# Another order of the first block's steps, with 39 unread products of the identity between TensorE's first steps

## The chip, the cores and the metric

The kernel runs on one core of a Trainium2 chip. The metric is the device time of one execution, in microseconds (us). The engines are TensorE (PE in the profile, PEld its weight loads), VectorE (DVE), ScalarE (ACT), GpSimd (POOL) and SyncE (SP), which issues most DMA transfers.

## The reference

q, k and v have the shape [8, 8, 576, 64] (batch, heads, tokens, width). Attention stays within chunks of 64 tokens; its result, as x of 4608 tokens by 512, goes through a feed-forward layer with 2048 inner columns, mish and no bias.

```python
scores = scale * np.matmul(q_c, k_c.transpose(0, 1, 2, 4, 3))
scores = scores - np.max(scores, axis=-1, keepdims=True)
attn = np.exp(scores)
attn = attn / (np.sum(attn, axis=-1, keepdims=True) + 1e-09)
out = np.matmul(attn, v_c)
...
h = x @ w_in
sp = np.where(h > 20.0, h, np.log1p(np.exp(np.minimum(h, 20.0))))
g = h * np.tanh(sp)
return (g @ w_out).astype(np.float32)
```

All of it is fp32. The kernel keeps nearly that precision in the feed-forward layer by splitting each operand in an upper part, rounded to a shorter type that TensorE multiplies in one pass (fp32r), and a lower part, the difference. A product is then three products of parts.

## The kernel before, in words

The tokens are taken in pairs of 64-token chunks of two batches; two pairs make a block of 512 tokens by 512. The first block is special: the weights have to be loaded, split and kept while it runs, and the attention of the first two pairs has to be done before anything can be multiplied by `w_in`. Later blocks run as a steady stream of products, in which sums of operands save some of the products.

A pair `j` passes through these steps. `load_qk` (L278) and `load_v` (L286) load it. `a_scores` is a run of small products (`small_mm`, L295, 64x64, `s<-k,q`). `a_max` (L321), `a_sub` (L333), `a_inverse` (L388 to L390) and `a_norm` (L395) are softmax on VectorE; `a_exp` (L342) is on ScalarE. `a_transpose` (L406, `pt<-ident,p`) turns p over with the identity `ident` on TensorE, `a_copy` (L416, `ps<-pt`) brings it to SBUF on ScalarE, `a_values` (L295, `av<-ps`) multiplies by v. `a_hi` (L446) and `a_lo` (L449) split the result into the parts of `x_first`. For the first two pairs each step is done for one half at a time: `a_scores 0 1` is pair 0, second half.

A weight `n` passes through `load` (L107), `scale` (L120 and L125, ACT), `bits` (L139, DVE; L143 stores a copy), `hi` (L164, ACT) and `lo` (L167, DVE); `keep` (L176, L177) writes the split weight to memory for the later blocks.

The feed-forward layer of the first block: `up i` (L524, `h<-x_first,wi`) makes 128 of the 2048 inner columns for 512 tokens with 12 products; the first of them is done in two halves of 256 tokens, `up0A` (pair 0) and `up0B` (pair 1). `mish i` (L537) follows on ACT, `gh` and `gl` (L546, L548, L552) split the result, and `fill i` issues the down products (`down_mm`, L562, `o<-wo,gl` and `o<-wo,gh`) into the accumulators of `w_out`, which `open` makes room for. The steps `x`, `s_load`, `s_adds`, `s_hi` and `s_lo` prepare the next block's operands.

What sets the order is a string written out by hand, `ORDER`. `first_block` takes its steps one by one and calls `atom`, which emits each step's instructions. An engine executes its own instructions in the order of emission; between engines, only data and buffers order them. The steps after `at n` don't run there, but beside products of the next block.

Of the kernel before, what the change touches and what calls it, by code (L numbers as in the profile page):

```python
# [9 lines left out]
F32 = mybir.dt.float32  # L10
# [7 lines left out]
P = 128  # L18
CHUNK = 64
# [4 lines left out]
def kernel(  # L24
# [34 lines left out]
    at = ctx.enter_context(tc.tile_pool(name="at", bufs=3))  # L59
# [204 lines left out]
    st = {}  # L264
# [248 lines left out]
    it = {}  # L513
# [41 lines left out]
    fill = []  # L555
# [108 lines left out]
    }  # L664

    ORDER = """
        qk0, a_scores 0 0, a_max 0 0, rooms, v0, a_sub 0 0, a_exp 0 0, a_scores 0 1, a_max 0
        1, load 0, load 1, qk1, load 3, scale 0, a_inverse 0 0, a_sub 0 1, a_norm 0 0, a_exp
        0 1, a_T 0 0, bits 0, load 4, hi 0, a_scores 1 0, a_inverse 0 1, a_copy 0 0, lo 0,
        a_norm 0 1, v1, a_max 1 0, scale 1, a_sub 1 0, a_V 0 0, a_hi 0 0, bits 1, a_exp 1 0,  # L670
        load 2, a_T 0 1, a_copy 0 1, a_lo 0 0, scale 3, a_inverse 1 0, a_scores 1 1, a_max 1
        1, a_sub 1 1, a_V 0 1, a_hi 0 1, hi 1, a_norm 1 0, a_lo 0 1, up0A, a_T 1 0, a_exp 1
        1, a_inverse 1 1, scale 4, a_norm 1 1, scale 2, a_copy 1 0, a_T 1 1, bits 3, load_qk
        0, a_copy 1 1, load 5, hi 3, lo 1, keep 0, bits 2, a_V 1 0, a_hi 1 0, a_lo 1 0, a_V
        1 1, load 6, a_hi 1 1, a_lo 1 1, open, scale 5, scores 0, bits 5, up0B, mish 0, hi
        2, hi 5, bits 4, up1, lo 2, load 7, hi 4, gh 0, gl 0, lo 3, load_v 0, mish 1, max 0,
        lo 5, scale 6, fill 0, gh 1, up 2, lo 4, mish 2, scale 7, fill 1, gh 2, bits 6, gl
        1, sub 0, hi 6, bits 7, gl 2, load 8, lo 6, hi 7, lo 7, up 3, load 9, keep 1, exp 0,
        fill 2, up 4, scale 8, inverse 0, fill 3, mish 3, up 5, bits 8, gh 3, norm 0, T 0,
        load 10, gl 3, scale 9, bits 9, load 11, load_qk 1, hi 8, fill 4, mish 4, gh 4, copy  # L680
        0, lo 8, V 0, gl 4, hi 9, lo 9, fill 5, scale 10, mish 5, scale 11, up 6, up 7, bits
        10, gh 5, raw 0, bits 11, mish 6, gl 5, scores 1, hi 10, gh 6, load 12, hi 11, lo
        10, mish 7, lo 11, load_v 1, load 13, scale 12, up 8, keep 2, max 1, sub 1, gl 6,
        mish 8, exp 1, fill 6, bits 12, gh 7, scale 13, up 9, hi 12, inverse 1, fill 7, load
        14, gl 7, norm 1, bits 13, lo 12, gh 8, load_qk 2, gl 8, T 1, fill 8, copy 1, V 1,
        hi 13, scale 14, lo 13, raw 1, load 15, bits 14, load 16, up 10, mish 9, gh 9,
        scores 2, max 2, mish 10, load_v 2, sub 2, fill 9, gl 9, scale 15, hi 14, bits 15,
        lo 14, exp 2, up 11, hi 15, inverse 2, gh 10, load 17, keep 3, fill 10, norm 2, up
        12, gl 10, scale 16, T 2, load_qk 3, lo 15, x 0 0, x 0 3, x 0 4, mish 11, bits 16,
        scale 17, fill 11, copy 2, mish 12, hi 16, gh 12, bits 17, gh 11, load 18, V 2, up  # L690
        13, lo 16, x 0 2, x 0 5, gl 11, gl 12, hi 17, raw 2, scores 3, fill 12, keep 4, lo
        17, max 3, sub 3, up 14, mish 13, scale 18, bits 18, x 0 1, x 1 1, hi 18, exp 3, lo
        18, load_v 3, keep 5, s_load 1, inverse 3, fill 13, up 15, s_load 0, x 0 8, gh 13,
        mish 14, gh 14, gl 13, norm 3, mish 15, s_adds 0, keep 6, s_hi 0, x 0 6, s_load 2,
        gl 14, T 3, fill 14, ops 2, copy 3, s_lo 0, gh 15, x 1 0, gl 15, x 0 7, s_adds 1, V
        3, raw 3, x 1 2, fl 0, x 1 3, x 1 4, x 1 5, x 0 9, keep 7, ops 3, fl 1, x 1 8, at 0,
        fill 15, x 1 9, x 1 7, at 1, fl 2, fl 3, fl 4, s_hi 1, at 2, fl 5, load_qk 4, fl 6,
        x 1 6, at 3, s_lo 1, x 0 10, at 4, s_load 3, x 1 10, at 5, fl 7, st 0, at 6, at 7,
        st 1, at 8, at 9, s_adds 2, s_adds 3, at 10, s_hi 3, s_hi 2, s_lo 2, at 11, at 12,
        at 13, s_lo 3, at 14, at 15, at 16, at 17, at 18, at 19, at 20, at 21, at 22, at 23  # L700
    """

    BY_SCALAR = (2, 4, 6, 7, 8, 10, 12, 13, 14,)
# [61 lines left out]
    def first_block():  # L765
# [644 lines left out]
```

## Time and profile before

| | us |
|---|---|
| three runs, median | 815.48 |
| three runs, lowest to highest | 814.03 to 815.96 |
| profiled execution, its own time | 815.17 |
| profiled execution, span from the first to the last instruction | 813.4 |
| TensorE busy in the span | 789.2 (97%) |
| VectorE busy | 546.5 (67%) |
| ScalarE busy | 462.8 (57%) |
| mean granted clock of TensorE | 0.998 |

The rows read from the trace all come from the one profiled execution; 1.8 us of its time lie outside its span. Times in them count from the span's start. A row of a timeline is a run of equal instructions of one engine: its start, its length, and in brackets the time for which the engine stood idle before it and what ended that. A row with many matmuls in sequence divides into one matmul's share of it, not its duration, because they overlap. [...] "DMA share" is the mean busy share of the core's 16 DMA engines.

### The profile page before, as it was taken

The page shows a single profiled execution, that of the slowest core. Times are in us where ns is not written, and L with a number is a line of the kernel's source. Part 1 is how long each engine was busy: PE and PEld are TensorE (multiplying, and loading weights), DVE is VectorE, ACT ScalarE, POOL GpSimd, SP SyncE. Part 2 cuts the span into 40 slices and gives each one's busy share as a digit, 9 for nine tenths or more (in the row PEclk, how much of TensorE's full clock was granted, in tenths as well). Part 3 has the DMA queues.
Part 4 walks back from the last instruction along what each step waited for, and adds up shares of the span by engine and source line. Part 5 has one row for each costly group of instructions (what it writes and reads, how often), then busy time and mean ns, then how long its engine had stood idle before and what let it go on. Part 6 is the DMA issues. An engine that isn't in the chain of part 4 may idle for free.

```text
span 813.4 us, 16433 instructions
## 1 busy us (share of the span) xinstructions
PE 789.2 (97%) x6376; PEld 680.2 (84%) x6376; DVE 546.5 (67%) x834; ACT 462.8 (57%) x694; POOL 0.7 (0%) x6
## 2 busy tenths in 40 slices
PE   4799999999999999999999999999999999999998
PEld 3677877788888888888899998888999988888887
DVE  6678889726557686676679854555698813348875
ACT  5797985535444544666645645666556534445543
POOL 0000000000000000000000000000000000000000
PEclk9999999999999999999999999999999999999999
DMA  8788888875777786988767688776576876666764
GB/s 324 264 292 326 311 286 318 287 265 206 270 263 227 220 298 189 357 298 283 234 171 210 194 266 276 252 243 200 164 209 185 232 217 195 193 193 190 212 195 129
DMA packets 101581, 196.12 MB, mean 241 GB/s; under 512 B 10112, under 2 KB 26496, under 8 KB 99456
## 3 DMA queue, kind: packets, MB, share of 16 engines
q1 hardware_dynamic: 100896, 194.29, 74.9%
q8 instruction: 51, 0.84, 0.4%
q10 hardware_dynamic: 608, 0.79, 0.3%
q14 instruction: 26, 0.21, 0.1%
HBM read 152.04 MB, written 42.99 MB: 240 GB/s over the span
## 4 chain that ended last, share of the span: by engine, by line
PE 85%; DMA 5%; ACT 4%; DVE 3%; issue 1%; SPq 0%; ACTq 0%
PE x L832 21%; PE X L1261 11%; PE v L832 11%; PE Z L1261 6%; PE y L832 6%; PE Y L1261 3%; PE X_a L1213 3%; PE X L1213 3%; PE Z L1213 3%; PE av L295 2%; PE s L295 2%; DMA wst<-in_w_out 2%; PE pt L406 1%; PE Y L1213 1%; PE o_(1, 1)_0_2768 L562 1%
## 5 line engine op out<-in xcount | busy, mean ns | idle before, releaser
L1166 ACT CAST gh<-g 128x512 fp32r<-128x512 f32 x168 | 103.5, 621 | 93.1 <-PE X L1261 29.9
L1169 DVE TENSOR_TENSOR gl<-g,gh 128x512 fp32r<-128x512 f32 x168 | 115.1, 689 | 49.0 <-ACT gh L1166 45.4
L832 PE MATMUL x<-x_T,w 128*128 128x512 f32 x390 | 97.5, 392 | 0.8 <-DMA w<-wa 0.8
L832 PEld LDWEIGHTS x<-x_T,w 128*128 128x128 f32 x390 | 72.5, 188 | 16.5 <-issue 1.2
L844 DVE TENSOR_TENSOR g<-v,g 128x512 f32<-128x512 f32 x48 | 33.0, 690 | 72.7 <-ACT g L1144 41.6
L537 ACT ACTIVATE g<-g 128x512 f32<-128x512 f32 x72 | 44.9, 631 | 59.3 <-DVE g L844 59.1
L524 PE MATMUL h<-x_first,wi 128*128 128x512 f32 (+1 forms) x204 | 48.7, 391 | 1.3 <-ACT x_first L446 0.7
L832 PE MATMUL x<-x_T,late 128*128 128x512 f32 x186 | 46.0, 391 | 0.0
L524 PEld LDWEIGHTS h<-x_first,wi 128*128 128x128 f32 x204 | 37.5, 195 | 9.9 <-ACT x_first L446 0.8
L1261 PE MATMUL X<-w,gh 128*128 128x256 f32 x288 | 40.5, 283 | 0.0
L832 PEld LDWEIGHTS x<-x_T,late 128*128 128x128 f32 x186 | 34.6, 188 | 7.0
L562 PE MATMUL o<-wo,gh 128*128 128x512 f32 x128 | 39.5, 390 | 0.0
L1261 PEld LDWEIGHTS X<-w,gh 128*128 128x128 f32 x288 | 37.2, 192 | 0.1
L844 DVE TENSOR_TENSOR g<-y,g 128x512 f32<-128x512 f32 x24 | 16.3, 680 | 30.2 <-PE y L832 29.6
L832 PE MATMUL v<-x_B,w 128*128 128x512 f32 x138 | 35.4, 395 | 0.3 <-DMA w<-wa 0.3
L1144 ACT COPY g<-x 128x512 f32<-128x512 f32 x24 | 14.1, 589 | 36.6 <-PE x L832 36.6
L832 PE MATMUL y<-x_B,w 128*128 128x512 f32 x126 | 31.8, 395 | 0.0
L1261 PE MATMUL X<-late,gh 128*128 128x256 f32 x224 | 31.5, 283 | 0.0
L832 PE MATMUL x<-x_B,w 128*128 128x512 f32 x126 | 31.5, 392 | 0.0
L832 PEld LDWEIGHTS v<-x_B,w 128*128 128x128 f32 x138 | 25.4, 188 | 6.4 <-issue 0.7
L832 PE MATMUL v<-x_T,w 128*128 128x512 f32 x120 | 29.6, 390 | 0.1
L1261 PEld LDWEIGHTS X<-late,gh 128*128 128x128 f32 x224 | 28.9, 192 | 0.1
(213 smaller groups left out, 1732.3 us busy)
## 6 DMA issues: line engine op xcount, KB each, us to landing
w<-wa SPq DMA_DIRECT2D x150, 256.0 KB, 3.8
w<-wb SPq DMA_DIRECT2D x94, 256.0 KB, 2.9
late<-wa SPq DMA_DIRECT2D x74, 256.0 KB, 3.3
late<-wb SPq DMA_DIRECT2D x74, 256.0 KB, 2.8
wst<-in_w_in SPq DMA_DIRECT2D x16, 512.0 KB, 5.2
wst<-in_w_out SPq DMA_DIRECT2D x16, 512.0 KB, 6.0
v<-in_v SPq DMA_DIRECT2D x16, 512.0 KB, 6.4
wa<-a SPq DMA_DIRECT2D x6, 1024.0 KB, 4.1
```

The lines of the kernel that those rows point to most:

```text
L295: nc.tensor.matmul(o[h * CHUNK : (h + 1) * CHUNK, c, t - ts.start, g], lhsT=l[rows, t, 2 * g + h], rhs=r[rows, t, 2 * g + h], start=True, ...
L406: nc.tensor.transpose(out=d["pt", ts.start][:, t - ts.start, g], in_=d["p"][:, t, g].rearrange("p c k -> p (c k)"), identity=ident,)
L524: nc.tensor.matmul(h[:, cols], lhsT=wi[i // 2][:, i % 2 * 2 + kt // 2, w_, kt % 2], rhs=x[:, x_, kt, cols], start=(n == 0), stop=(n == 3 * ...
L537: nc.scalar.activation(out=out_, in_=in_, func=AF.Mish)
L562: nc.tensor.matmul(acc[t], lhsT=g[:, t * P : (t + 1) * P], rhs=wo[f // 2][:, f % 2, part], start=(f == 0 and n == 0), stop=(f == NF - 1 an ...
L832: nc.tensor.matmul(o, lhsT=t[:, w_, kt], rhs=x[x_][:, kt], start=(start and i == 0), stop=(i == 5), skip_group_check=not start,)
L844: nc.vector.tensor_tensor(out=z, in0=o, in1=z, op=ALU.add)
L1144: nc.scalar.copy(out=z["G22"], in_=o)
L1166: nc.scalar.copy(out=d["gh"], in_=g)
L1169: nc.vector.tensor_tensor(out=d["gl"], in0=g, in1=d["gh"].bitcast(F32), op=ALU.subtract)
L1213: nc.tensor.matmul(o, lhsT=d[g][:, t * P : (t + 1) * P], rhs=w__, start=(first and n == 2), stop=(u == NU - 1 and g == "gl"), skip_group_c ...
L1261: nc.tensor.matmul(o, lhsT=d[g][:, t * P : (t + 1) * P], rhs=w_[:, part], start=(k in (0, 1, 3) and u == 0 and t % 2 == 0 and n == 0), sto ...
```

## The change

A function `unread` is added; each call issues three plain fp32 products of the 128x128 identity with its own first 64 columns, into a PSUM tile that nothing reads (the tile that `h_1` gets later, once `h_0` exists). Thirteen calls stand in the new list, 39 products. In the same list most steps of the first block have another place. No step is removed, and none of the other functions changes. In the changed kernel the lines behind the added function have numbers that are 15 to 18 higher; the products themselves are L643.

```diff
@@ -629,6 +629,21 @@
     rooms = {}
     opened = {}
 
+    idle = {}
+
+    def unread():
+        if "h" not in idle:
+            idle["h"] = ps_h.tile([P, TOK], F32, name="unread", tag="h")
+        o = idle["h"]
+        if 0 in it:
+            if 1 not in it:
+                it[1] = {"h": ps_h.tile([P, TOK], F32, name="h_1", tag="h")}
+            o = it[1]["h"]
+        for _ in range(3):
+            nc.tensor.matmul(
+                o[:, 0:CHUNK], lhsT=ident, rhs=ident[:, 0:CHUNK], start=True, stop=True
+            )
+
     def room(n):
         if n not in rooms:
             rooms[n] = xo_p.tile([P, 2, 2, H, CHUNK], F32, name=f"room_{n}", tag="x")
@@ -648,6 +663,7 @@
         "up1": lambda: up(1, last="w"),
         "open": open_accumulators,
         "rooms": lambda: (room(0), room(1)),
+        "unread": unread,
     }
     TOP_ATTENTION = {
         "a_scores": (a_scores, ("h0", "h0")),
@@ -664,40 +680,42 @@
     ORDER = """
-        qk0, a_scores 0 0, a_max 0 0, rooms, v0, a_sub 0 0, a_exp 0 0, a_scores 0 1, a_max 0
...
+        qk0, a_scores 0 0, a_max 0 0, load 0, a_sub 0 0, a_scores 0 1, unread, unread,
+        unread, unread, rooms, v0, a_exp 0 0, unread, scale 0, unread, qk1, load 3, a_max 0
...
```

Rows of the list tell little, so here is the order of TensorE's instructions at three places. "x18" counts instructions of the program; a plain fp32 product is one instruction here and two pairs of weight load and matmul in the trace.

The first steps on TensorE. `s_0_0` and `s_0_1` are the scores of pair 0's halves, `pt` its transposes, `av` its values, `room` the buffers of pair 1's q, k and v. Before:

```order
L295 MATMUL s_0_1_168<-k_0_138,q_0_137 64x64 x16
L406 MATMUL pt_0_0_203<-ident_81,p_0_165 128x128 x4
L295 MATMUL s_1_0_213<-room_1_163,room_0_162 64x64 x16
L295 MATMUL av_0_0_245<-ps_0_234,room_0_162 64x64 x16
L406 MATMUL pt_0_1_268<-ident_81,p_0_165 128x128 x4
L295 MATMUL s_1_1_281<-room_1_163,room_0_162 64x64 x16
L295 MATMUL av_0_1_301<-ps_0_234,room_0_162 64x64 x16
```

and in the change:

```order
L295 MATMUL s_0_1_165<-k_0_138,q_0_137 64x64 x16
L643 MATMUL unread_182<-ident_81 128x64 x18
L295 MATMUL s_1_0_223<-room_1_196,room_0_195 64x64 x16
L406 MATMUL pt_0_0_240<-ident_81,p_0_163 128x128 x4
L643 MATMUL unread_182<-ident_81 128x64 x3
L295 MATMUL av_0_0_256<-ps_0_250,room_0_195 64x64 x16
L643 MATMUL unread_182<-ident_81 128x64 x9
L406 MATMUL pt_0_1_292<-ident_81,p_0_163 128x128 x4
L295 MATMUL s_1_1_298<-room_1_196,room_0_195 64x64 x16
L295 MATMUL av_0_1_318<-ps_0_250,room_0_195 64x64 x16
```

The first 18 unread products stand between pair 0's scores and pair 1's, and `s_1_0` comes ahead of `pt_0_0`; twelve more stand around `av_0_0`.

The next steps on TensorE, up to the second half of the first up product (`h_0`, 256 columns) and what follows it; `s_2` are the scores of pair 2, from the buffer `qk`. Before:

```order
L524 MATMUL h_0_322<-x_first_262,wi_0_211 128x256 x12
L406 MATMUL pt_1_0_335<-ident_81,p_1_243 128x128 x4
L406 MATMUL pt_1_1_352<-ident_81,p_1_243 128x128 x4
L295 MATMUL av_1_0_370<-ps_1_350,room_1_163 64x64 x16
L295 MATMUL av_1_1_389<-ps_1_350,room_1_163 64x64 x16
L295 MATMUL s_2_0_416<-qk_2_358 64x64 x32
L524 MATMUL h_0_322<-x_first_262,wi_0_211 128x256 x12
```

and in the change:

```order
L643 MATMUL unread_182<-ident_81 128x64 x3
L524 MATMUL h_0_361<-x_first_273,wi_0_245 128x256 x12
L406 MATMUL pt_1_0_381<-ident_81,p_1_284 128x128 x4
L643 MATMUL h_1_386<-ident_81 128x64 x6
L406 MATMUL pt_1_1_404<-ident_81,p_1_284 128x128 x4
L295 MATMUL av_1_0_409<-ps_1_391,room_1_196 64x64 x16
L295 MATMUL av_1_1_427<-ps_1_391,room_1_196 64x64 x16
L295 MATMUL s_2_0_446<-qk_2_355 64x64 x32
L524 MATMUL h_0_361<-x_first_273,wi_0_245 128x256 x12
```

Nine unread products are between these steps; the rest keeps its order.

TensorE, near the end of the first block: `av_4` are pair 4's values, `s_5` pair 5's scores, `h_13` an up product, `o` the down products. Before:

```order
L562 MATMUL o_0_3_532<-wo_5_103,gl_0_10_1108 128x512
L562 MATMUL o_0_3_532<-wo_5_103,gh_0_10_1076 128x512 x2
L295 MATMUL av_4_0_1162<-ps_4_1148,v_4_1033 64x64 x32
L524 MATMUL h_13_1195<-x_first_262,wi_12_1053 128x512 x12
L295 MATMUL s_5_0_1220<-qk_5_1121 64x64 x32
L562 MATMUL o_0_0_520<-wo_5_103,gl_0_11_1213 128x512
```

and in the change:

```order
L562 MATMUL o_0_3_575<-wo_4_102,gh_0_9_1095 128x512 x2
L295 MATMUL av_4_0_1179<-ps_4_1170,v_4_1031 64x64 x32
L562 MATMUL o_0_0_563<-wo_5_103,gl_0_10_1168 128x512
L562 MATMUL o_0_0_563<-wo_5_103,gh_0_10_1098 128x512 x2
L562 MATMUL o_0_1_567<-wo_5_103,gl_0_10_1168 128x512
L562 MATMUL o_0_1_567<-wo_5_103,gh_0_10_1098 128x512 x2
L562 MATMUL o_0_2_571<-wo_5_103,gl_0_10_1168 128x512
L562 MATMUL o_0_2_571<-wo_5_103,gh_0_10_1098 128x512 x2
L562 MATMUL o_0_3_575<-wo_5_103,gl_0_10_1168 128x512
L562 MATMUL o_0_3_575<-wo_5_103,gh_0_10_1098 128x512 x2
L295 MATMUL s_5_0_1229<-qk_5_1106 64x64 x32
L524 MATMUL h_13_1264<-x_first_273,wi_12_1072 128x512 x12
```

Between `av_4` and `s_5` there stood the up product `h_13`; now there are the down products of one inner column block, and `h_13` comes behind `s_5`.

On SP's queue the first loads are in another order too: a weight and then v stand ahead of pair 1's q and k, where v and two weights stood, and the second weight now has seven transfers between the first one and itself.

## Rows read from the trace of the kernel before

**Rows 1.** The page's first part: busy time of each engine, share, number of instructions.

```profile
PE 789.2 (97%) x6376; PEld 680.2 (84%) x6376; DVE 546.5 (67%) x834; ACT 462.8 (57%) x694; POOL 0.7 (0%) x6
```

**Rows 2.** Windows of the span; a line begins with its window, us; last PEclk, DMA share, GB/s.

```profile
10.00:20.00 10.00, 6.74 (x146) 5.58 (x147) 9.79 (x20) 8.57 (x16) 0.00 (x0) 1.00 1.00 361
20.00:30.00 10.00, 5.83 (x152) 5.07 (x151) 6.28 (x12) 6.37 (x11) 0.00 (x0) 0.96 1.00 365
28.00:33.00 5.00, 5.00 (x21) 4.30 (x22) 1.53 (x3) 2.14 (x4) 0.00 (x0) 0.66 0.99 369
...
40.00:120.00 80.00, 79.05 (x707) 63.63 (x705) 68.03 (x78) 71.12 (x81) 0.00 (x0) 1.00 0.88 302
120.00:160.00 40.00, 35.66 (x273) 27.98 (x274) 35.39 (x58) 23.79 (x36) 0.00 (x0) 1.00 0.90 308
160.00:800.00 640.00, 640.00 (x4937) 559.29 (x4936) 409.87 (x639) 338.51 (x533) 0.00 (x0) 1.00 0.74 229
```

**Rows 3.** Waits of TensorE, whole span: line, released by, us in total, times, longest.

```profile
PE pt L406 <- ACT p L342: 3.4, 1, 3.4
PE s L295 <- issue: 3.3, 1, 3.3
PE pt L406 <- DVE p L395: 2.3, 2, 1.6
PE av L295 <- ACT ps L416: 1.8, 2, 1.7
PE s L295 <- DVE x_first L449: 1.2, 1, 1.2
...
PE h L524 <- ACT x_first L446: 0.7, 1, 0.7
PE h L524 <- DVE x_first L449: 0.4, 1, 0.4
```

**Rows 4.** Timeline of TensorE, 4 to 30 us: start, length, operation, count, idle before it.

```profile
5.19 2.36 PE L295 MATMUL s<-k,q 64*64 64x64 f32 x64 [5.19 <-DMA k<-in_k]
10.93 1.09 PE L406 MATMUL pt<-ident,p 128*128 128x128 f32 x4 [3.37 <-ACT p L342]
...
13.86 1.11 PE L406 MATMUL pt<-ident,p 128*128 128x128 f32 x4
...
16.68 0.65 PE L295 MATMUL av<-ps,room 64*64 64x64 f32 x32
18.03 1.21 PE L524 MATMUL h<-x_first,wi 128*128 128x256 f32 x8 [0.71 <-ACT x_first L446]
...
20.26 0.60 PE L406 MATMUL pt<-ident,p 128*128 128x128 f32 x4
...
22.35 1.18 PE L295 MATMUL av<-ps,room 64*64 64x64 f32 x64 [0.19 <-ACT ps L416]
23.56 1.16 PE L295 MATMUL s<-qk 64*64 64x64 f32 x63
27.99 0.27 PE L295 MATMUL s<-qk 64*64 64x64 f32 x1 [3.27 <-issue]
```

**Rows 5.** DMA queues by kind, whole span and 25 to 27 us: packets, MB, share.

```profile
q8 instruction: 51, 0.84, 0.4%
...
q8 instruction: 1, 0.02, 2.8%
```

**Rows 6.** Timeline of TensorE, 27 to 40 us.

```profile
28.18 8.76 PE L524 MATMUL h<-x_first,wi 128*128 128x256 f32 x36
```

**Rows 7.** Timeline of TensorE, 50 to 82 us.

```profile
53.87 1.03 PE L406 MATMUL pt<-ident,p 128*128 128x128 f32 x8
...
61.52 5.60 PE L524 MATMUL h<-x_first,wi 128*128 128x512 f32 x24
```

**Rows 8.** Timeline of VectorE, 5 to 30 us: the last split of the second pair.

```profile
23.84 1.28 DVE L449 TENSOR_TENSOR x_first<-av,x_first 128x512 fp32r<-128x512 f32 x2
```

More of the change, by code (lines that the diff above doesn't have):

```diff
@@ L666 @@
     ORDER = """
-        qk0, a_scores 0 0, a_max 0 0, rooms, v0, a_sub 0 0, a_exp 0 0, a_scores 0 1, a_max 0
[L668 to L700, printed above, removed]
+        qk0, a_scores 0 0, a_max 0 0, load 0, a_sub 0 0, a_scores 0 1, unread, unread,
+        unread, unread, rooms, v0, a_exp 0 0, unread, scale 0, unread, qk1, load 3, a_max 0
@@ new lines @@
+        1, a_sub 0 1, a_inverse 0 0, bits 0, a_norm 0 0, a_exp 0 1, a_scores 1 0, a_T 0 0,
+        hi 0, unread, a_copy 0 0, a_inverse 0 1, a_V 0 0, a_hi 0 0, a_max 1 0, unread,
+        a_norm 0 1, unread, a_sub 1 0, load 1, a_exp 1 0, unread, lo 0, a_T 0 1, a_lo 0 0,
+        a_scores 1 1, scale 3, a_copy 0 1, a_V 0 1, a_inverse 1 0, a_max 1 1, a_sub 1 1,
+        scale 1, a_hi 0 1, a_norm 1 0, load 4, a_exp 1 1, unread, load 2, scale 2, v1,
+        load_qk 0, scale 4, a_lo 0 1, up0A, a_inverse 1 1, bits 1, hi 1, a_T 1 0, unread,
@@ new lines @@
+        load 5, a_copy 1 0, unread, a_norm 1 1, bits 2, bits 3, load 6, lo 1, a_T 1 1, a_V 1
+        0, a_copy 1 1, a_V 1 1, a_hi 1 0, a_lo 1 0, scores 0, a_hi 1 1, a_lo 1 1, max 0,
+        up0B, hi 3, hi 2, up1, lo 2, open, bits 4, scale 5, mish 0, up 2, bits 5, hi 5, lo
+        3, hi 4, gh 0, gl 0, lo 4, load 7, mish 1, up 3, fill 0, lo 5, keep 1, fill 1,
+        load_v 0, scale 6, sub 0, gh 1, gl 1, exp 0, bits 6, scale 7, inverse 0, hi 6, load
+        8, norm 0, mish 2, bits 7, hi 7, load 9, gh 2, lo 6, gl 2, fill 2, scale 8, lo 7,
@@ new lines @@
+        load_qk 1, T 0, mish 3, up 4, scale 9, bits 8, gh 3, fill 3, mish 4, gl 3, up 5,
+        bits 9, hi 8, fill 4, mish 5, copy 0, V 0, load 10, gh 4, load 11, lo 8, hi 9, gl 4,
+        scale 10, up 6, raw 0, scores 1, up 7, keep 0, lo 9, fill 5, gh 5, bits 10, hi 10,
+        lo 10, max 1, load 12, mish 6, load_v 1, scale 11, up 8, gl 5, keep 2, mish 7, fill
+        6, up 9, sub 1, gh 6, bits 11, scale 12, gl 6, load 13, bits 12, hi 11, lo 11, mish
+        8, load 14, fill 7, exp 1, gh 7, inverse 1, norm 1, hi 12, T 1, scale 13, keep 3, gl
@@ new lines @@
+        7, gh 8, lo 12, bits 13, copy 1, fill 8, V 1, scale 14, load_qk 2, load 15, hi 13,
+        bits 14, load 16, up 10, raw 1, load_v 2, scores 2, gl 8, mish 9, mish 10, hi 14, lo
+        13, fill 9, scale 15, max 2, lo 14, sub 2, exp 2, gh 9, bits 15, gh 10, inverse 2,
+        load 17, load_qk 3, norm 2, hi 15, scale 16, up 11, gl 9, up 12, T 2, bits 16, x 0
+        0, lo 15, fill 10, gl 10, copy 2, hi 16, x 0 2, scale 17, V 2, fill 11, raw 2, load
+        18, lo 16, scores 3, mish 11, up 13, keep 4, x 0 3, mish 12, keep 6, up 14, bits 17,
@@ new lines @@
+        gh 12, hi 17, gh 11, max 3, x 0 4, sub 3, x 0 5, gl 11, gl 12, scale 18, bits 18, hi
+        18, exp 3, lo 17, lo 18, fill 12, keep 7, inverse 3, fill 13, x 0 1, mish 13, up 15,
+        gh 13, norm 3, s_load 1, mish 14, gh 14, s_load 0, gl 13, load_v 3, s_adds 0, T 3,
+        fill 14, x 0 8, ops 2, s_hi 0, keep 5, copy 3, V 3, s_load 2, x 0 6, s_lo 0, mish
+        15, gl 14, fl 0, s_adds 1, x 1 0, load_qk 4, x 0 7, gh 15, raw 3, ops 3, gl 15, x 1
+        3, x 1 1, fl 1, s_load 3, x 1 4, at 0, x 1 2, s_hi 1, x 1 5, x 0 9, x 1 9, x 1 7,
@@ L701 @@
+        fill 15, at 1, fl 2, fl 3, fl 4, x 1 8, at 2, fl 5, fl 6, at 3, s_lo 1, x 1 6, at 4,
+        x 0 10, x 1 10, at 5, fl 7, st 0, at 6, at 7, st 1, at 8, at 9, s_adds 3, s_adds 2,
+        s_hi 3, s_hi 2, at 10, s_lo 2, at 11, at 12, at 13, s_lo 3, at 14, at 15, at 16, at
+        17, at 18, at 19, at 20, at 21, at 22, at 23
     """
```

## The prediction

> **What bounds the kernel now.** I read the shares of the engines first, then the stages, the waits of TensorE, and the timeline of the stage in which the waits stand. TensorE is busy for 789.2 of 813.4 us [rows 1]. The table by stages shows where the other 24 us are [rows 2]: from 160 to 800 us the engine is busy for 640.00 of 640 us, so an order of first steps can gain nothing there; from 120 to 160 it is idle for 4.34 us, from 40 to 120 for 0.95, and most of the rest lies in the first 30 us. TensorE therefore sets the end, and every microsecond that it loses early is lost for good; one that the first block saves is kept if no later wait takes it.
>
> The waits of TensorE [rows 3, 4] name the losses: 5.2 us for the first k, which the change leaves alone (q is still the first transfer of SP's queue, and k is loaded by ACT's); 3.4 for the first softmax; 1.2, 0.7, 0.7 and 0.4 while softmax and splitting of the first two pairs go on; and 3.3 that no instruction ends ("issue"), inside 64 equal products. The last is the odd one. The timeline [rows 4] shows it: 63 of the 64 products `s<-qk` run in 1.16 us from 23.56, and the 64th starts at 27.99, 3.27 us late, though it needs nothing that its 63 neighbours did not have. In 25 to 27 us one packet of the queue named "instruction" is moved [rows 5], and it is the only one between 24 and 28. Over the whole run that queue moves 51 packets of 0.84 MB in all, 16 KB each [rows 5], against 12,752 matmuls and weight loads of TensorE [rows 1]: about 250 to a packet. So I read the 3.27 us as the engine waiting for its own code, behind data transfers that keep all 16 DMA engines busy (share 1.00 from 10 to 30 us) [rows 2].
>
> It costs twice. [...] The next matmuls say the same: 36 of them take 8.76 us [rows 6], where 24 of the wide ones take 5.60 at the full clock [rows 7] and 12 narrow ones at 1.21 for 8 take 1.8 [rows 4], together 7.4: 1.4 us lost. Stall and clock: 3.27 + 1.7 = 5.0 us.
>
> [...]
>
> **The change: what goes.** Each unread product shows up, like the other plain fp32 products, as two pairs of weight load and matmul (16 calls of `small_mm` are 32 rows): 39 products are 78 pairs. They stand ahead of the place where the code ran out. That was behind 347 pairs (64+4+32+32+4+32+32+8+4+4+4+64+63 on TensorE's timeline, its first and last rows in [rows 4]). In the new order the 347th pair is the 17th of the second half of `av_1`, and one packet, 128 pairs, lies between the 23rd pair of `s_1_1` and it. The trace does not show when a packet is asked for. If it is asked for one packet ahead, that was at 22.35 (the 219th pair) and the code was there at 27.99: 5.6 us. In the new order those 128 pairs are the rest of `s_1_1` and `av_0_1`, 18 unread pairs, `up0A`, the transposes and one and a half of `av_1`: 6.1 us of work by rows 4 and the prices below, and up to 1.8 us of waits that were there before. That is 6.1 to 7.9 us against 5.6: the stall goes, narrowly. -5.0 us.
>
> **What comes: the unread products.** The trace of before has no 128x128 by 64 product. The nearest rows are the transposes, with the same `ident` and twice the columns: 4 in 1.08 to 1.11 us, 0.27 each, before the clock rises [rows 4], 8 in 1.03, 0.128 each, after [rows 7]. Upper end: those. Lower end: the 64x64 pairs, 2.36 us for 64 early and 1.16 later, 0.037 and 0.018 [rows 4]. I take 0.2 and 0.1, nearer to the transposes, which load the same weights.
>
> The first 36 pairs stand behind `s_0_1`, that is at 7.55, in the wait of 3.37 us that ended at 10.93. All at the low rate and the upper price they end at 17.3, all at the high rate at 12.2. The rows of before show the low rate at 13.86 and the high one at 16.68 [rows 4], after an engine that had stood until 10.93; now it works from 5.19 on, so I let half of them run at each rate: 36 x 0.15 = 5.4, to 13.0. That is 2.0 us beyond the cover. The other 42 pairs stand behind it: 42 x 0.1 = 4.2 us. Of these 6.2 us the other waits up to `s_2` (1.2, 0.7, 0.4, 0.7, 0.2: 3.2 us [rows 3, 4]) cover about half, 1.6, since softmax and splitting begin later when their products do. An earlier full clock gives back about 0.5 on each of the four groups that ran from 10.93 to 14.97 (first and last 1.09 and 1.11 us, against 0.60 to 0.65 at 16.68 and 20.26 [rows 4]), 1.9. Net, 6.2 - 1.6 - 1.9 = 2.7 us: `s_2` ends at 24.72 + 2.7 = 27.4 instead of 28.2 with the stall, and `up0B` starts there. Its inputs are no later: the last split on VectorE ended at 25.1 [rows 8], and it shifts with the `av_1` before it.
>
> [...]
>
> **What is moved.** On SP's queue the first weight goes ahead of the first v and the second one behind seven others, so that q and k of pair 1 stand behind two transfers of 512 KB where three stood. At 10 us the queue moved about 360 GB/s [rows 2], so `s_1_0` has its data 1.4 us earlier; it has no wait in rows 3, so I count nothing. `up1`, `up 2` and `up 3` now come ahead of the first `down`, whose inputs need `mish` on ACT in between: a cover, worth nothing while hardly a wait shows there (0.95 us idle in 40 to 120). Scores and transposes of later pairs stand earlier among the products; the two waits of 1.6 and 1.7 us (the longest of their lines [rows 3]) are for `p` and `ps` of pair 4 and end with work of VectorE (DVE) and ScalarE (ACT). Those two engines get the same work in another order, so the waits may go or grow: between -2.5 and +2.5 us; I take -0.3.
>
> **The sum.** Against the profiled execution, 815.17 us (0.31 below the median of 815.48): -5.0 + 2.7 - 0.3 = -2.6, so 812.6; against the median 812.9. I put it at **812.6 us**. The bounds of the unknown price: at the transposes' 0.27 and 0.128, all of the first 36 at the low rate, 17.3 - 10.9 + 5.4 = 11.8 us of pairs, of which the covers leave 6.7 to 8.3: +1.4 to +3.0 with the rest of the sum, 818.2 at most; at 0.037 and 0.018 less than 2 us of pairs, all covered, and -5.0 - 1.9 - 0.3 = -7.2: 808.0.
>
> **Rivals.**
> - *The unread products are dear.* At the transposes' price, half of the first 36 at each rate, they end at 14.7; 3.8 + 5.4 = 9.2 us of pairs, less 1.6 to 3.2 and 1.9: 4.1 to 5.7, so -1.2 to +0.4: 814.0 to 815.6, some 814.7. For it: the weights are those of the transposes. Against: half the columns.
> - *The late waits go too.* In 40 to 160 us 5.29 us are idle [rows 2]. If pair 4's softmax comes early enough, 2.5 of them go: about 810. Against it: the first `down`s start later in the new order and the lead is spent by then.
> - *The code runs out elsewhere (slower).* All later boundaries move too. By the count of pairs one now falls within `s_5_0`, with its request just ahead of `av_4_0`; between them stand only those short pairs and 12 `o`. Before, the 12 wide matmuls of `h_13` stood between the two bursts, now they come after. If the queue of data is deep when it is asked for, TensorE stops there at about 115 us, for as much as it did at 24.7: 3.27 and 1.7 of clock. It decides if the transfer needs more than the 5 or so us that lie between; then the end is 812.6 + 5.0 = 817.6. Against: the DMA share there is 0.90, not 1.00 [rows 2], and none of the other boundaries of before shows such a wait [rows 3].
> - *The change does not do what its words say.* The products stand there, but the stall stays: it is inside `av_1_1`, or it has another cause than code and meets the same 64 products again. Then 3.27 and 1.7 remain, less what the covers take: 814 to 817.6. [...]
>
> **How the numbers follow.** Forecast 0.50 (its own range 811.0 to 814.0), dear products 0.25, late waits 0.09, code elsewhere 0.08, stall kept 0.08. About 0.3%, 2.45 us, is what a measurement can tell from no change: faster is below 813.0. The forecast lies mostly under it (0.40 of its 0.50), with the late waits and a little of the dear products: 0.52. Slower is above 817.9: half of the code rival, and a little of dear products and stall: 0.08. The rest, 0.40, is the same. The range leaves out the ends: 809.5 to 816.0.
>
> **What would show it.** Right: no "issue" wait in the row of `s<-qk`, granted clock 1.00 from 28 to 33 us, `up0B` starting near 27.4, 36 unread pairs done by 13, and the same 640 of 640 us later. Wrong: `up0B` later than 29 (dear products), an "issue" wait of over 1 us anywhere on TensorE, or more than 5.3 us idle between 40 and 160.

## The result, and the profile after

| | before | the change |
|---|---|---|
| median on the same chip, us | 814.58 (6 runs) | 819.84 (6 runs, 818.77 to 823.03) |
| ratio, 95% interval | | 1.0082 (1.0061 to 1.0102) |
| profiled execution, us | 815.17 | 819.40 |
| its span, us | 813.4 | 817.6 |
| start of the second half of the first up product (`up0B`), us | 28.18 [rows 6] | 33.45 |
| span behind that start, us | 785.2 | 784.2 |

The change makes the kernel slower by 0.8%, 5 to 8 us by the interval; the medians lie 5.3 us apart, the profiled executions 4.2. The forecast was 812.6 with a range up to 816.0, so it missed, on the wrong side.

The page's first part of the change; [rows 1] answer to it:

```profile
PE 802.7 (98%) x6454; PEld 694.8 (85%) x6454; DVE 547.2 (67%) x834; ACT 463.1 (57%) x694; POOL 0.7 (0%) x6
```

TensorE is busy for 13.5 us more than before, with 78 more weight loads and as many more matmuls (6454 against 6376): the 39 products are there, two pairs each. The stages, to be held against [rows 2] (of the last three columns the first, "PEclk", is the granted clock as a share of the full one, the second the DMA share):

```profile
10.00:20.00 10.00, 10.00 (x101) 9.53 (x101) 4.65 (x10) 1.52 (x3) 0.00 (x0) 1.00 1.01 369
20.00:30.00 10.00, 9.92 (x115) 9.27 (x115) 5.92 (x13) 7.13 (x14) 0.00 (x0) 1.00 0.13 50
28.00:33.00 5.00, 4.87 (x131) 4.36 (x134) 4.90 (x11) 4.50 (x9) 0.00 (x0) 1.00 0.46 135
...
40.00:120.00 80.00, 75.72 (x691) 60.80 (x690) 63.69 (x71) 68.72 (x76) 0.00 (x0) 1.00 0.92 323
120.00:160.00 40.00, 38.92 (x289) 30.94 (x289) 37.87 (x62) 27.43 (x40) 0.00 (x0) 1.00 0.85 285
```

The losses of the first 30 us are gone: 10.00 and 9.92 us busy where there were 6.74 and 5.83. But busy with what? TensorE's timeline from 4 to 45 us, to be held against [rows 4, 6]:

```profile
7.34 7.94 PE L643 MATMUL unread<-ident 128*128 128x64 f32 x36
15.21 1.13 PE L295 MATMUL s<-room,room 64*64 64x64 f32 x32
16.27 1.11 PE L406 MATMUL pt<-ident,p 128*128 128x128 f32 x4
17.18 1.38 PE L643 MATMUL unread<-ident 128*128 128x64 f32 x6
...
19.55 4.10 PE L643 MATMUL unread<-ident 128*128 128x64 f32 x18
23.44 1.06 PE L406 MATMUL pt<-ident,p 128*128 128x128 f32 x4
...
26.23 0.88 PE L643 MATMUL unread<-ident 128*128 128x64 f32 x6
...
28.89 0.60 PE L406 MATMUL pt<-ident,p 128*128 128x128 f32 x4
29.32 1.45 PE L643 MATMUL h<-ident 128*128 128x64 f32 x12
...
32.41 1.11 PE L295 MATMUL s<-qk 64*64 64x64 f32 x64
33.45 9.88 PE L524 MATMUL h<-x_first,wi 128*128 128x256 f32 x48
```

From 7.34 until `up0B` TensorE stands idle for only 0.13 us in all. The unread pairs take 7.94 + 1.38 + 4.10 + 0.88 + 1.45 = 15.75 us. The first 60 of them (36, 6 and 18) cost 0.22 to 0.23 each, the last 18 cost 0.12 to 0.15. The pair did not change; the level of the engine did. Four transposes take 1.11 and 1.06 us at 16.27 and 23.44, and 0.60 at 28.89: the lower level until behind 24.4, and the upper one, about 1.8 times as quick, by 28.9; the six pairs at 26.23 are already quick, at 0.15 each. The level is read here as the clock, because equal products were slow too where the "PEclk" column did fall: at 0.66 [rows 2] 36 of them took 8.76 us [rows 6], and 36 of the 48 at 33.45 take 7.4. In the kernel before four took 0.60 at 20.26 and the products of `av` were already quick at 16.68, 32 in 0.65 [rows 4]. The "PEclk" column shows 1.00 throughout, here from 10 to 30 us, and in [rows 2] from 10 to 20, where the transposes at 10.93 and 13.86 ran at the low rate too. In this stretch equal rows tell the level and the column does not.

What was forecast of the stall came true: `s<-qk` is one run of 64 in 1.11 us, no line of the waits ends in "issue", the clock from 28 to 33 us is 1.00 where it was 0.66 [rows 2], and the 36 products that took 8.76 us behind the stall now are the first 36 of 48 that take 9.88. The late waits kept their sum and changed their names:

```profile
PE h L524 <- ACT z L537: 2.4, 3, 1.3
PE pt L406 <- DVE p L395: 2.3, 2, 2.0
```

From 40 to 160 us TensorE is idle for 4.28 + 1.08 = 5.36 us, where it was 5.29 [rows 2]: the waits near 121 and 127 us shrank, and others came between 49 and 105.

The long unread run has a second effect. VectorE stands still for its scores (4.17 us here, and 3.60 again at 25.63), and with it SP, which waits for a piece of weight that VectorE makes. From VectorE's timeline in the change:

```profile
16.41 0.69 DVE L321 TENSOR_REDUCE m<-s 128x8 f32<-128x512 f32 x1 [4.17 <-PE s L295]
```

Between 14.88 and 29.87 us SP issues nothing, and the DMA share from 20 to 30 us is 0.13, where it was 1.00. Transfers that were done by 30 us come later.

### The profile page after: what moved, and what is told of

It reads as the page before. It is cut to its first block, busy times and chain, and to the rows that moved or that the text cites. A ratio compares the mean times of both kernels' runs of the same rounds, so it can differ in the third digit from the quotient of the medians.

```text
span 817.6 us, 16589 instructions
## 1 busy us (share of the span) xinstructions
PE 802.7 (98%) x6454; PEld 694.8 (85%) x6454; DVE 547.2 (67%) x834; ACT 463.1 (57%) x694; POOL 0.7 (0%) x6
## 4 chain that ended last, share of the span: by engine, by line
PE 82%; DMA 8%; DVE 5%; ACT 3%; issue 1%; SPq 0%; ACTq 0%; DVEq 0%
PE x L850 20%; PE X L1279 11%; PE v L850 10%; PE Z L1279 6%; PE y L850 5%; PE Y L1279 3%; PE X_a L1231 3%; PE X L1231 3%; PE Z L1231 3%; DMA wst<-in_w_in 2%; DMA wst<-in_w_out 2%; PE pt L406 2%; PE s L295 2%; PE unread L643 2%; PE av L295 2%; DMA wa<-a 2%
## 5 line engine op out<-in xcount | busy, mean ns | idle before, releaser
L850 PEld LDWEIGHTS v<-x_B,w 128*128 128x128 f32 x138 | 25.4, 188 | 6.5 <-DVE zb L862 1.2
L1279 PEld LDWEIGHTS X<-late,gh 128*128 128x128 f32 x224 | 28.9, 192 | 0.1
```

Of the source, the lines that this page charges most:

```text
L850: nc.tensor.matmul(o, lhsT=t[:, w_, kt], rhs=x[x_][:, kt], start=(start and i == 0), stop=(i == 5), skip_group_check=not start,)
L1279: nc.tensor.matmul(o, lhsT=d[g][:, t * P : (t + 1) * P], rhs=w_[:, part], start=(k in (0, 1, 3) and u == 0 and t % 2 == 0 and n == 0), sto ...
```

## The experiments

The start of `up0B` is a fair mark: in all runs below the profiled span ends 782.4 to 787.2 us behind it, so that it tells large differences and not those of 1 or 2 us. Each experiment is read by that start and by its time. Ratios are to the kernel before on the same chip; of each median the before of its own group stands beside it.

**The order alone, and the products alone.** The first takes the thirteen calls out of the change's list; the second puts them into before's list.

```diff
-        qk0, a_scores 0 0, a_max 0 0, load 0, a_sub 0 0, a_scores 0 1, unread, unread,
-        unread, unread, rooms, v0, a_exp 0 0, unread, scale 0, unread, qk1, load 3, a_max 0
+        qk0, a_scores 0 0, a_max 0 0, load 0, a_sub 0 0, a_scores 0 1, rooms, v0, a_exp 0 0, scale 0, qk1, load 3, a_max 0
...
```

and for the second

```diff
-        ...a_scores 0 1, a_max...
+        ...a_scores 0 1, unread, unread, unread, unread, unread, unread, a_max...
-        ...a_V 0 0...
+        ...unread, a_V 0 0...
-        ...a_T 0 1...
+        ...unread, unread, unread, a_T 0 1...
-        ...up0A, a_T 1 0...
+        ...unread, up0A, a_T 1 0, unread, unread...
```

> The change's order without its 39 unread products (13 calls taken out). Theory 1 (the products cost: 78 pairs at 0.22 us while the clock stays low, some 10 us more than the waits cover): without them up0B starts near 24 to 28 us instead of 33.45. By the count of pairs the code boundary is back at the 63rd pair of s_2, so if code loading follows the count, an 'issue' wait of 2 to 4 us comes back there and the time is 812 to 816; if it does not come back, 808 to 811. Theory 2 (the order costs, the products are covered): as the change, 818 to 820.

> The order of before, with the 39 unread products between the same steps as in the change. Theory 1: as slow as the change or slower, 818 to 821; TensorE's products still at the lower rate at 20 us; no 'issue' wait at s_2. Theory 2: the products are covered and the stall gone, 810 to 813.

Measured: the order alone 813.35 us, ratio 0.9995 (0.9982 to 1.0008; before 813.40); the products alone 821.64, ratio 1.0103 (1.0084 to 1.0122), a little above the 818 to 821 expected. The whole loss is the products'; the order by itself is worth nothing that can be told. TensorE's timelines, first of the products alone:

```profile
7.42 7.94 PE L643 MATMUL unread<-ident 128*128 128x64 f32 x36
...
23.63 1.06 PE L406 MATMUL pt<-ident,p 128*128 128x128 f32 x4
...
35.74 7.17 PE L524 MATMUL h<-x_first,wi 128*128 128x256 f32 x36
```

The same 7.94 us for 36 pairs, transposes at the low rate at 23.63, `up0B` 7.6 us later than in before. Of the order alone:

```profile
11.51 1.11 PE L406 MATMUL pt<-ident,p 128*128 128x128 f32 x4
...
21.82 1.91 PE L406 MATMUL pt<-ident,p 128*128 128x128 f32 x8
...
24.92 1.11 PE L295 MATMUL s<-qk 64*64 64x64 f32 x62
27.45 0.27 PE L295 MATMUL s<-qk 64*64 64x64 f32 x2 [1.43 <-issue]
27.66 9.88 PE L524 MATMUL h<-x_first,wi 128*128 128x256 f32 x48
```

The "issue" wait is back, by 1.43 us (2 to 4 were expected) and at the 63rd pair of `s<-qk`, as the count of pairs wants it (it stood at the 64th in before). And the clock rises late here too, with no unread product in the list: transposes still at 0.28 each at 11.51, and 1.91 for 8 at 21.82. So it is not the unread products alone that keep it down. In before's list `s_1_0` and `av_0_0` ran back to back ahead of the rise; in the new list a transposition stands between them. The last experiment below tries that.

**Where does the pair's price come from?** Sixteen columns instead of 64; and the products on a quarter of the array.

```diff
-                o[:, 0:CHUNK], lhsT=ident, rhs=ident[:, 0:CHUNK], start=True, stop=True
+                o[:, 0:16], lhsT=ident, rhs=ident[:, 0:16], start=True, stop=True
```

> The change with 16 columns in each unread product in place of 64. If loading the 128x128 identity sets a pair's time, it stays near 0.2 us and the kernel at 817 to 820. If the columns do, a pair falls to 0.1 us or less, the 78 pairs to 6 to 8 us, and the time to 812 to 815.

Measured: 823.03, ratio 1.0103 (1.0068 to 1.0137; before 814.87). The time is above the 817 to 820 expected, but the interval overlaps that of the change.

```profile
7.47 7.86 PE L643 MATMUL unread<-ident 128*128 128x16 f32 x36
```

A quarter of the columns, and 36 pairs take 7.86 instead of 7.94 us, 0.22 each. In the change the 36 weight loads fill 7.75 us of PEld. So it is the weights that set the price, not the columns, as far as 16 and 64 columns tell. In the change a pair costs 0.12 us at the upper level (12 in 1.45) and 0.22 at the lower one (36 in 7.94), about twice as much.

The quarter products take rows 0 to 63 or 64 to 127 of the identity as both operands, in two PSUM banks:

```diff
+            rows = slice(c * CHUNK, (c + 1) * CHUNK)
+            nc.tensor.matmul(
+                o[c][h * CHUNK : (h + 1) * CHUNK, 0:CHUNK],
+                lhsT=ident[rows, 0:CHUNK], rhs=ident[rows, 0:CHUNK], start=True, stop=True,
+            )
```

> The change with each unread product 64x64 by 64, on a quarter of the array, instead of 128x128 by 64: as many pairs, at 0.04 to 0.1 us each. Theory 1: 3 to 6 us of pairs in place of 15.8, half of them in waits; no stall at s_2, since the count of pairs is the change's; 808 to 812, and the full clock some us earlier than at 26. Theory 2: 818 to 820 again.

Measured: 812.55, ratio 0.9989 (0.9973 to 1.0006; before 813.40); 808 to 812 were expected.

```profile
7.06 1.31 PE L647 MATMUL unread<-ident 64*64 64x64 f32 x36
...
21.59 1.05 PE L406 MATMUL pt<-ident,p 128*128 128x128 f32 x4
...
26.14 9.89 PE L524 MATMUL h<-x_first,wi 128*128 128x256 f32 x48
```

The same number of pairs at the same places costs 1.31 us where it cost 7.94, `up0B` starts at 26.14, and the loss is gone. The theory of the products' own time holds. But the transposes at 21.59 still ran at the low rate (1.05 us for four), although TensorE was busy for 9.50 of the 10 us from 10 to 20 us.

**Half of the products.** Only the first six calls, behind pair 0's scores.

```diff
-        ...a_T 0 0, hi 0, unread, a_copy 0 0...
+        ...a_T 0 0, hi 0, a_copy 0 0...
-        ...a_max 1 0, unread, a_norm 0 1, unread, a_sub 1 0, load 1, a_exp 1 0, unread, lo 0...
+        ...a_max 1 0, a_norm 0 1, a_sub 1 0, load 1, a_exp 1 0, lo 0...
-        ...a_exp 1 1, unread, load 2...
+        ...a_exp 1 1, load 2...
-        ...a_T 1 0, unread, load 5, a_copy 1 0, unread, a_norm 1 1...
+        ...a_T 1 0, load 5, a_copy 1 0, a_norm 1 1...
```

> The change with only the first six calls, 18 of its 39 unread products, behind pair 0's scores. Theory 1 (a pair costs 0.22 us at the low clock; what the waits don't cover is lost): 36 pairs still end near 15.2, but 7.8 us of pairs behind them go, of which 1 to 3 come back as waits; up0B starts at 27 to 29 and the end follows it by 784 to 785 us of span: 813 to 815.5. If the loss were due to the first 18 alone, 817 to 820.

Measured: 815.83, ratio 1.0014 (0.9994 to 1.0033; before 814.87).

```profile
7.38 7.94 PE L643 MATMUL unread<-ident 128*128 128x64 f32 x36
...
30.44 9.88 PE L524 MATMUL h<-x_first,wi 128*128 128x256 f32 x48
```

`up0B` at 30.44 is a little later than expected, 27 to 29: of the 7.8 us of pairs left out, 4.8 come back as waits or at the low rate. The first 18 products cost as in the change.

**Is the stall a wait for code?** In before's order, 21 of the quarter products (42 pairs) in the wait behind pair 0's scores.

```diff
-        qk0, a_scores 0 0, a_max 0 0, rooms, v0, a_sub 0 0, a_exp 0 0, a_scores 0 1, a_max 0
+        qk0, a_scores 0 0, a_max 0 0, rooms, v0, a_sub 0 0, a_exp 0 0, a_scores 0 1, unread, unread, unread, unread, unread, unread, unread, a_max 0
```

> The order of before, with 21 of those small products (42 pairs) in one place, behind pair 0's scores, in the wait of 3.4 us. If the 3.27 us stall is a wait for code that follows the count of pairs, the boundary moves 42 pairs forward, into s_2's first half, its request by over 5 us, and the stall goes, with the low clock behind it: 809 to 811.5. If the stall has another cause it stays at the 64th s_2 pair: 814 to 816.

Measured: 813.60, ratio 1.0005 (0.9989 to 1.0020; before 813.40).

```profile
12.99 1.13 PE L295 MATMUL s<-room,room 64*64 64x64 f32 x32 [1.35 <-issue]
...
24.65 1.16 PE L295 MATMUL s<-qk 64*64 64x64 f32 x64
25.74 7.17 PE L524 MATMUL h<-x_first,wi 128*128 128x256 f32 x36
...
43.12 2.49 PE L524 MATMUL h<-x_first,wi 128*128 128x512 f32 x5 [1.94 <-ACT wi L164]
```

`s<-qk` is whole again, as expected, and `up0B` starts 2.4 us earlier than in before. But a wait of 1.35 us that no instruction ends has come up at 12.99, ahead of `s_1_0`, and the kernel is not faster: at 43.12 TensorE waits 1.94 us for a weight's upper part, behind which the granted clock is 0.65 from 43.12 to 48 us. The span behind `up0B` is 787.2 us, where before had 785.2: most of what the earlier start gained is lost again. The forecast of 809 to 811.5 for this run was wrong for that reason, as far as its one trace tells.

**Does dense work raise the clock?** In before's order, 8 products of 512 columns in the same wait. VectorE first copies the identity four times side by side into a tile of `w_out` that is loaded much later; that step (`wide`) stands at the head of the list.

```diff
+        for _ in range(8):
+            nc.tensor.matmul(idle["o"], lhsT=idle["w"][:, 0:P], rhs=idle["w"], start=True, stop=True)
```

> The order of before, with 8 unread products of 512 columns (split type, identity four times side by side, copied by VectorE into a tile of w_out that is loaded later) in the wait of 3.4 us behind pair 0's scores. [...] If dense products raise the clock where the narrow ones did not, the transposes that ran at 0.27 us each at 10.93 and 13.86 run at 0.13 to 0.15, by 13.86 at the latest; up0B starts up to 1.5 us earlier, 810 to 813.5. If the clock rises when it did in before whatever stands there, the transposes stay at 0.27 and the time at 812.5 to 815.

Measured: 813.25, ratio 0.9978 (0.9958 to 0.9997; before 814.87).

```profile
7.24 3.64 PE L643 MATMUL unread<-wo 128*128 128x512 f32 x8
10.72 0.60 PE L406 MATMUL pt<-ident,p 128*128 128x128 f32 x4
...
17.73 2.93 PE L524 MATMUL h<-x_first,wi 128*128 128x256 f32 x12 [0.71 <-ACT x_first L446]
...
23.73 1.04 PE L295 MATMUL s<-qk 64*64 64x64 f32 x55 [0.30 <-DMA qk<-in_k]
27.22 0.38 PE L295 MATMUL s<-qk 64*64 64x64 f32 x9 [2.46 <-issue]
```

The four transposes at 10.72 take 0.60 us, where they took 1.09 at 10.93: behind eight dense products of 3.64 us the clock was up, where behind 7.94 us of narrow ones it was not. The dense products differ from the narrow ones in two things, the columns and the type (fp32r, one row of the timeline to a product, 8 for 8, where a plain product has two, 36 for 18); no run here parts the two. What it brings is small: behind waits of 1.87 and 0.71 us, 12 products of `up0A` take 2.93 us at 17.73, the low rate again. Its windows:

```profile
10.00:20.00 10.00, 6.79 (x149) 5.64 (x148) 9.76 (x20) 8.37 (x15) 0.00 (x0) 0.87 1.04 373
20.00:30.00 10.00, 6.86 (x152) 6.11 (x151) 6.10 (x11) 6.20 (x10) 0.00 (x0) 0.84 1.02 353
```

0.87 and 0.84 are read here, in a run in which the clock had risen and fell. The stall tells its place in passing: it comes behind 55 products of `s<-qk`, and 8 pairs were put ahead. 63 - 8 = 55: it follows the count of instructions, not the data.

The "instruction" queue, read in windows of 0.2 us, points to code as well. In each run with such a wait one packet of that queue is moved shortly ahead of its end, and TensorE goes on 2.2 to 2.6 us behind it, the wait of 1.35 us in the run with the 21 quarter products included (the last two runs are those at the end of this section):

| run | packet moved within, us | TensorE goes on, us |
|---|---|---|
| before | 25.4 to 25.6 | 27.99 |
| before, once more | 25.0 to 25.2 | 27.50 |
| the order alone | 25.0 to 25.2 | 27.45 |
| 21 quarter products | 10.6 to 10.8 | 12.99 |
| 8 dense products | 24.8 to 25.0 | 27.22 |
| the order alone, `s_1_0` put back | 26.0 to 26.2 | 28.55 |

**The deciding run: dense products ahead of the change's own.**

```diff
-        ...a_scores 0 1, unread, unread...
+        ...a_scores 0 1, dense, unread, unread...
```

(`dense` is the loop of the run before, in the change's list; `wide` stands at its head here too.)

> The change with the 8 products of 512 columns in front of its 39 narrow ones. The 8 end near 10.9 and raise the clock as they did alone. If the narrow products hold a clock that is up, their 78 pairs cost 0.12 us each, 9.4 instead of 15.8; up0B starts near 28 to 30 and the time is 812.5 to 816. If they neither raise nor hold it, the clock falls again among the first 36 of them, the pairs go back to 0.22, and the 3.6 us come on top of the change's: up0B at 34 to 37, 819 to 823.

Measured: 814.02, ratio 0.9992 (0.9978 to 1.0006; before 814.15), as in the first case expected.

```profile
7.25 3.78 PE L657 MATMUL dense<-wo 128*128 128x512 f32 x8
10.82 4.41 PE L643 MATMUL unread<-ident 128*128 128x64 f32 x36
...
15.79 0.66 PE L406 MATMUL pt<-ident,p 128*128 128x128 f32 x4
16.28 0.78 PE L643 MATMUL unread<-ident 128*128 128x64 f32 x6
...
17.75 2.22 PE L643 MATMUL unread<-ident 128*128 128x64 f32 x18
...
21.71 0.88 PE L643 MATMUL unread<-ident 128*128 128x64 f32 x6
...
24.79 1.45 PE L643 MATMUL h<-ident 128*128 128x64 f32 x12
...
28.93 9.89 PE L524 MATMUL h<-x_first,wi 128*128 128x256 f32 x48
```

Eight more products on top of the change, 3.78 us more work, and the ratio to before falls from 1.0082 to 0.9992, by 0.9%. The same 36 pairs now take 4.41 us instead of 7.94, 0.12 each, and 18 take 2.22 instead of 4.10. So the narrow products did not raise the clock in the change, but with the clock up ahead of them it stayed up here. All 78 pairs take 4.41 + 0.78 + 2.22 + 0.88 + 1.45 = 9.74 us, 6.0 less than in the change. `up0B` starts 4.52 us earlier although 3.78 us of work were added: 8.3 us in all were the price of the low level, 6.0 on the pairs and 2.3 on the steps between them.

**A version faster than both.** First v of pair 0 behind q and k of pair 1, with the quarter products; then the dense eight in front as well, in place of the first call (its edit is not shown).

```diff
-        unread, unread, rooms, v0, a_exp 0 0, unread, scale 0, unread, qk1, load 3, a_max 0
+        unread, unread, rooms, a_exp 0 0, unread, scale 0, unread, qk1, v0, load 3, a_max 0
...
```

> The change with the small unread products, and pair 0's v loaded behind q and k of pair 1 instead of ahead of them. In the run with the small products TensorE waited 1.8 us for pair 1's k; with one 512 KB transfer less ahead that wait shrinks to about 0.4. If nothing else is late, up0B starts 1 to 1.5 us earlier and the time is 810.5 to 812; if v is late for av_0_0 or the weights bound what follows, as small_unread, 812 to 813.

> A try at a kernel faster than both: the change's order, v of pair 0 behind pair 1's q and k, the 8 dense products first and the small ones (39 less 3) in place of the narrow ones. If the clock is up from 10.6 us and no wait lets it fall, the transposes, scores and up0A that ran at half rate up to 18 to 24 us in the other runs of this order save 2 to 3 us, up0B starts at 23 to 25 and the end follows: 808.5 to 811. If something else is late there (p, the weights' parts, qk), up0B stays at 25 to 26 and the time at 811 to 813.

Measured: 812.29, ratio 0.9976 (0.9954 to 0.9997; before 814.87); with the dense ones 811.75, ratio 0.9960 (0.9943 to 0.9976; before 814.15). The first is the second case expected: the wait for pair 1's k shrank from 1.79 to 0.45 us, but `up0B` starts at 25.41, only 0.7 us earlier than with the quarter products alone. The last is faster than before by 0.4%. Its start of `up0B` is that of the better case expected, its time that of the other. Its timeline:

```profile
12.55 0.66 PE L406 MATMUL pt<-ident,p 128*128 128x128 f32 x4
...
24.89 9.89 PE L524 MATMUL h<-x_first,wi 128*128 128x256 f32 x48
```

Transposes at 0.66 for four by 12.55, `up0B` at 24.89. Only 0.5 us earlier than in the run without the dense products (25.41): `p`, `ps` and `x_first` of the first pairs are late next, with six waits of 0.16 to 0.70 us. The span behind is 785.5.

**Why does the order alone raise the clock late, and how typical was the first profile?** Two last runs: the order alone with pair 1's first scores put back behind pair 0's first transposition, and the kernel before once more.

```diff
-        ...a_scores 1 0, a_T 0 0, hi 0...
+        ...a_T 0 0, a_scores 1 0, hi 0...
```

> The change's order without the unread products, and pair 1's first scores behind pair 0's first transposition, as before had them, so that s_1_0 and av_0_0 run back to back again. If that row of 64 short products is what raised the clock in before, four transposes take about 0.6 us by 17 us at the latest, up0B starts 2 to 3 us earlier than the 27.66 of the order alone, unless the stall is longer, and the time is 810.5 to 813. If something else delays the rise, the transposes stay at 1.05 to 1.11 beyond 20 us and the time at 812.5 to 814.5.

> The kernel before, unchanged, for a second profile. If the stall of the first profile was a typical one, the issue wait is 2.5 to 3.5 us again, at the 64th product of s<-qk, and the span 812 to 814. If it varies with the data queues, the wait is 0 to 2 us at the same product and the span 809 to 812; in both cases the transposes at 10.9 and 13.9 run at the low rate and those at 20 at the high one.

Measured: 813.83 for the first, ratio 0.9998 (0.9984 to 1.0012; before 814.25).

```profile
19.90 2.93 PE L524 MATMUL h<-x_first,wi 128*128 128x256 f32 x12 [0.70 <-ACT x_first L446]
22.63 1.44 PE L406 MATMUL pt<-ident,p 128*128 128x128 f32 x8
```

`s_1_0` and `av_0_0` stand together, at 12.67 and 13.58, and 12 products at 19.90 still take 2.93 us, the low rate; the 8 transposes at 22.63, with 1.44 us, are partly quick. So that pair of rows did not raise it here. The kernel before, once more, 814.17 us:

```profile
13.58 0.83 PE L406 MATMUL pt<-ident,p 128*128 128x128 f32 x4
...
17.74 2.93 PE L524 MATMUL h<-x_first,wi 128*128 128x256 f32 x12 [0.70 <-ACT x_first L446]
...
27.50 0.27 PE L295 MATMUL s<-qk 64*64 64x64 f32 x1 [2.68 <-issue]
```

The stall is 2.68 us, at the same product, where it was 3.27. The clock is up at 13.58, for part of the four transposes (0.83), and down again at 17.74: 12 products in 2.93, where 8 took 1.21 at the high rate [rows 4]. (The expectation had the low rate there at 13.9 and the high one at 20.) So in this thin stretch the level of before itself differs from one execution to the next, and what raises it between sparse products stays open. What is shown is the difference of dense and narrow filler: in all three runs with the dense eight the transposes behind them took 0.60 to 0.66 us by 15.8, in all four with narrow 128x128 products alone those before 24 took 1.05 us or more. Put into before's own list, the narrow products were followed by a later rise: four transposes still took 1.05 us at 30.55, where both profiles of before show some quick rows by 16.7.

## Why the prediction was wrong, by its own steps

- **"I let half of them run at each rate: 36 x 0.15 = 5.4, to 13.0", and 0.1 for the other 42.** This is the step that failed. All 36, plain products in a row, ran at the low rate, 7.94 us, to 15.2, and so did 24 of the other 42. Forecast for all 78 was 9.6 us; measured 15.75, 6.15 more. `up0B` came at 33.45 instead of 27.4, 6.05 later: about the failed term, since two other misses nearly cancel (next point). The prices themselves were near (0.22 and 0.12 for 0.2 and 0.1), and with the clock raised first the pairs took 9.74. What was wrong was that the engine's being busy would raise the clock: it was taken from the two rows at 13.86 and 16.68, with no regard to what kind of work stood ahead of the rise. The price leaned on transposes "which load the same weights"; they load `p` and stream the identity (in a row's name the weights stand last, as in `o<-wo,gl`), so only the size is the same.
- **Cover of 1.6 us, and 1.9 given back by an earlier full clock.** The first was too small: behind the wait of 3.37 us, which was counted apart, the waits of before up to `up0B` are 1.19 + 0.71 + 0.44 + 0.68 + 0.19 = 3.21 us without the stall, and all are gone, 1.6 more than counted. The second never came: the four groups took 1.06 to 1.13 us in the change. Together: 15.75 of pairs, less 3.37 + 3.21 = 6.58 and the stall of 3.27, is 5.9 us, of which the start shows 5.27.
- **-3.27 for the stall, with its cause.** Right: it moved by exactly 8 pairs with 8 pairs put ahead, is absent with 78, and ends 2.2 to 2.6 us behind a packet of instructions wherever it stands. The forecast counts a packet as 128 pairs; 12,752 matmuls and weight loads in 51 packets [rows 1, 5] are 125 pairs to a packet, and no run shows 128. What the runs show is the shift by 8 pairs and the time at which the packet was moved. One reading in it was off: 220 pairs end ahead of 22.35, so the 219th ran near 21.8, and the code took 6.2 us from there, not 5.6, which leaves hardly a margin against the 6.1 to 7.9 forecast. In the change those 128 pairs took some 7 us (25.1 to 32.1). The packet was moved at 25.4, 0.4 us behind the 219th pair, with the data queues nearly idle (share 0.13 from 20 to 30 us); in before, with a share of 1.00, it was moved 3.6 us behind it. That fits a request about one packet ahead, an estimate from these two times; no trace shows the request.
- **-1.7 for the clock behind it.** Right in kind, but no run shows a loss of 1.7 us. A granted clock of 0.66 over the 5 us from 28 to 33 [rows 2] makes 0.34 x 5 = 1.7, an estimate; what the runs show is 1.35: the 36 products behind `up0B` take 7.4 us in the change (36 of the 48 in 9.88) where it was 8.76 [rows 6]. Of the span behind `up0B` only 1.0 us came back (785.2 to 784.2), not 1.7 and 0.3.
- **-0.3 for late waits.** None: 5.36 us idle from 40 to 160 us against 5.29. With that and with `up0B` later than 29, two of the three signs of being wrong came.
- **The rivals.** The one on the slower side, code that runs out at `s_5_0`, didn't happen; no "issue" wait is left. "Dear products" had the direction but took the clock to be up for half of the first run and all of the rest. The upper bound, 818.2, let only the first 36 run at the low rate, and so was no bound: at 819.84 the time passed it.

The profiled execution of before was also dearer than the second: 3.27 us of stall against 2.68, and 815.17 us against medians of 813.40 to 814.87 in the groups of the experiments. So the -5.0 was taken from a larger case, by about 0.6 us as far as two executions tell.

## What to carry to other kernels

A busy TensorE is not yet a quick one. In these runs the clock was up behind 8 products of 512 columns (3.64 to 3.78 us, and four transposes behind them took 0.60 to 0.66), while products of 64 columns, each with its own weight load, kept the engine busy and were paid at the low rate (36 pairs in 7.94 us, and four transposes behind them took 1.06 to 1.11). So try dense filler first, and read the level behind it from equal rows. Price filler at the rate the clock has when it starts, and put it where a wait is longer than that. The stall amid equal products, with a packet of the instruction queue ahead of its end, moved with the count of instructions: 8 pairs ahead moved it by 8, and with 42 cheap ones (1.49 us) it was gone from there and a wait of 1.35 us stood at another place. So a few cheap ones ahead move it, but look at what is late next before counting it as gained.

## What was not expected of the hardware

- Narrow products did not raise a clock that was down, but it stayed up over them once it was: 0.12 to 0.15 us a pair for all 78 with eight dense products ahead, 0.22 to 0.23 for the first 60 without.
- A pair of weight load and matmul with 128x128 weights costs the same with 16 and with 64 columns, 0.22 us at the low level (36 in 7.86 and in 7.94).
- In all six stalls TensorE goes on 2.2 to 2.6 us after the lone packet of the instruction queue was moved. The packet itself came 3.6 us after the 219th pair with full data queues, and 0.4 us with nearly idle ones.
- The clock column of the profile reads 1.00 ahead of the first rise, where equal rows run at about half rate (from 10 to 20 us in the change: four transposes in 1.11 us, against 0.60 later).
- 3.78 us of work that nothing reads made the changed kernel 0.9% faster.
- The level in the first 25 us differs between executions of the same kernel; what raises it among sparse products is open, and with the new order alone it rose only behind 20 us, in both runs of it (12 products in 2.93 us at 19.09 and 19.90).
